# The last pair's V in 2 KB pieces on P's own partitions, P copied in two instructions, w_down in 2 KB pieces

## The chip, the core and the metric

The kernel runs on one core of a Trainium2 chip. The metric is device time in microseconds of one execution, lower is better; the time before is the median of three runs. All times inside a profile are counted from the span's start. TensorE (PE) multiplies, PEld is its weight load, VectorE (DVE), ScalarE (ACT) and GpSimd (POOL) compute, SyncE (SP) issues the DMAs.

## The reference

Two identical layers of decoding for four sequences with one new token each: a layer norm, attention with 32 query heads over 8 key/value heads and a cache of 4096 positions, then a layer norm and a gated MLP. The caches are the same in both layers.

```python
# B=4, D=512, Hq=32, Hkv=8, Sk=4096, Dh=128, F=1792, all bf16
def _A_ref(x, k_cache, v_cache, wq, wo):
    q = (x @ wq).reshape(B, Sq, Hq, Dh).transpose(0, 2, 1, 3)
    k = jnp.repeat(k_cache, 4, axis=1)
    v = jnp.repeat(v_cache, 4, axis=1)
    scores = jnp.einsum("bhqd,bhkd->bhqk", q, k) * (Dh ** -0.5)
    p = softmax(scores)
    o = jnp.einsum("bhqk,bhkd->bhqd", p, v)
    return o.transpose(0, 2, 1, 3).reshape(B, Sq, Hq * Dh) @ wo

def _B_ref(x, w_gate, w_up, w_down):
    h = sigmoid(x @ w_gate) * (x @ w_up)
    return h @ w_down

x = A_x
for _ in range(2):
    x = x + _A_ref(layernorm(x), A_k_cache, A_v_cache, A_wq, A_wo)
    x = x + _B_ref(layernorm(x), B_w_gate, B_w_up, B_w_down)
return x
```

## The kernel before

**Units and pairs.** One unit of attention is one layer, one sequence and one key/value head; there are 64, taken in pairs of two neighbouring heads, so 32 pairs (0 to 31). `ORDER` fixes the sequence of the pairs; the MLP of a sequence and its queries for the second layer (`pass_steps`) are strewn between the pairs at the places of `PLACES`. K and V of a unit are 1 MB each and lie in one of 12 slots of 128 partitions x 8 KB. Some K and V stay in their slots for the second layer (`RET`); the rest is loaded again, 98 loads in all.

**Loads.** All loads are issued by SP, in the order of `LOADS`, by `pump` (L382) as far as slots are free. Partition p of a slot gets the 32 cache rows 32p to 32p+31, one run of 8 KB (L402). The weights' loads are `wparts` (L363, issued at L388): w_o in eight parts, w_gate and w_up in four each, w_down in two parts of 7 x 128 rows, where partition p gets rows 128k + p, so that each run is one row of 1 KB. A wait of SP for a slot stands in its queue ahead of all later loads.

**One pair on the engines.** The main loop (L1172) runs over steps k = 0 to 32; step k computes the scores and the softmax of pair k and, behind it, the product with V of pair k - 1. The engines take their instructions in the order in which the loop emits them. For a pair g:
- `k_turn` (L848): DVE transposes the unit's K in its slot. `scores` (L863): PE multiplies with the queries into one PSUM bank, so that the scores of both units lie in 128 partitions x 256 columns.
- `smax` (L886, L890): DVE takes the maximum over the columns. `spread_max` (L897): PE spreads it. `softmax`: DVE reduces it over the partitions (L906, with a read of its accumulator), ACT takes the exponential (L914) into `pe`, POOL splits the sums (L928).
- `sums` (L937) and `inverse` (L947) give the reciprocal sums of the pair before.
- `ptrans`: PE transposes P into the bank `PT` (L959). There, of the 32 runs of 8 positions on a group of partitions, position (x, a) does not lie on the partition that holds its V row, so 16 copies of 32 partitions x 64 columns (x = 0 to 3, a = 0 to 3) move it: from partitions 32x to partitions 32a. For pairs 0 to 30 all 16 are ACT's (L982, into `pT`). For pair 31 the eight with x even are ACT's and the eight with x odd are DVE's (L974, into `pT_last`, which lies in a free slot): four of them at once, four put off into `later` until after the normalisation of pair 30.
- `pv` (L999): 32 products with V for each unit, eight behind each x. `pv_last` (L1027) does both units of pair 31 in one, 64 products, in the order of x; it waits for both V's slots and for the copies of each x.
- `normalise` (L1059): DVE multiplies the output by the reciprocal sums. `wo_mm` (L1077) and `wo_add` (L1097): the product with w_o, added to x.

At the end of step 30 stand the transposes and copies of pair 30's P, then the first scores of pair 31. Step 31 emits, in this order: the second scores of pair 31, `sums(30)`, `smax(31)`, one w_o product, `spread_max(31)`, `softmax(31)`, `inverse(30)`, `pv(60)`, `ptrans(31)`, `pv(61)`, `normalise(30)`. Step 32: `sums(31)`, `inverse(31)`, `pv_last`, the w_o product of pair 30, `normalise(31)`, the w_o product of pair 31.

**The MLP.** `wide_mm` (L676) computes gate or up transposed: the 128 hidden rows of block fc come out on the 128 partitions, from 128 columns of w_gate or w_up as stationary operand, four products for each block, 14 blocks. `down` (L795) and, in the last MLP, `down_rows` (L1299) multiply with w_down block by block; row p of block fc must be partition p of w_down's block fc. The last MLP, for all four sequences at once, follows the last w_o product: the layer norm (L507 to L555), `x_rows` (L1276), gate and up (112 products), the tanh, `down_rows`, and the output.

Of the kernel before, what the change touches and what calls it, by code (L numbers as in the profile page):

```python
# [6 lines left out]
ACTF = mybir.ActivationFunctionType  # L7
# [83 lines left out]
    "vkkvkkkkvv", "kkvkvvv", "kvk", "", "kvkvvvvkvvk", "", "kvkv", "",  # L91
    "", "kkvkvvkkkkvvkv", "kkvvv", "", "", "vvkkkvkkv", "", "vkvkv",
    "vvv",
)


# [110 lines left out]
def bass_interleave_layers__gqa_block_cached__glu_gated_glu__decode_kernel(  # L207
# [15 lines left out]
    REP = HQ // HKV  # L223
# [126 lines left out]
    for k, kinds in enumerate(LOADS):  # L350
        for o in range(2):
# [5 lines left out]
            if 2 * k + o >= 3 and w_small:  # L357
# [9 lines left out]
                         A_wo[n * REP * P:(n + 1) * REP * P, :].rearrange("(h p) n -> p h n", p=P)),  # L367
        "wg": lambda n: (wg_sb[:, n, :], B_w_gate[n * P:(n + 1) * P, :]),
        "wu": lambda n: (wu_sb[:, n, :], B_w_up[n * P:(n + 1) * P, :]),
        "wd": lambda n: (wd_sb[:, n * KH:(n + 1) * KH, :],  # L370
                         B_w_down[n * KH * P:(n + 1) * KH * P, :].rearrange("(k p) n -> p k n", p=P)),
    }
    assert KF == 2 * KH
    wkeys = {"wg": [f"wg{k}" for k in range(KD)], "wu": [f"wu{k}" for k in range(KD)], "wd": ["wd0", "wd1"]}
# [3 lines left out]

    def take():
        return free.pop(0)  # L380

    def pump():  # L382
        while loads:
            kind, n = loads[-1]
            if kind in wparts:
                loads.pop()
                dst, src = wparts[kind](n)
                S.dma("sp", (lambda dst, src: lambda e: e.dma_start(dst, src))(dst, src), f"wo{n}" if kind == "wo" else kind, writes=[f"{kind}{n}"])  # L388
                continue
            if not free:  # L390
                return
            loads.pop()
            s = take()
            _, b, u = seq[n]
            if kind == "k":
                where["kn", n] = s
                src = A_k_cache[b, u].rearrange("(p j) d -> p (j d)", p=P)
            else:
                where["v", b, u] = s
                src = A_v_cache[b, u].rearrange("(p j) d -> p (j d)", p=P)  # L400
            dst = slot[s][:, :]
            S.dma("sp", (lambda dst, src: lambda e: e.dma_start(dst, src))(dst, src), f"d{s}", writes=[f"s{s}"])  # L402
# [267 lines left out]
    def wide_mm(nb, which, f0, f1, M, mk):  # L670
        wsb, keys = ((wg_sb, wkeys["wg"]), (wu_sb, wkeys["wu"]))[which]
        fns = []
        for fc in range(f0, f1):
            for k in range(KD):
                fns.append(
                    (lambda fc, k: lambda e: e.matmul(  # L676
                        M[:, 64 + fc * nb:64 + (fc + 1) * nb],
                        lhsT=wsb[:, k, fc * P:(fc + 1) * P],
                        rhs=xc_bf[:, k, 0:nb],
                        start=(k == 0),  # L680
                        stop=(k == KD - 1),
                    ))(fc, k)
                )
        S.group("pe", fns, reads=["xcb"] + keys, writes=[mk])
# [264 lines left out]
            writes=[f"rden{p}"],  # L949
        )  # L950

    later = []

    def ptrans(g):
        p = g % 2
        fns = []
        for j in range(2):
            fns.append(
                (lambda j: lambda e: e.matmul(  # L959
                    PT[:, j * P:(j + 1) * P], lhsT=pe_sb[p][:, j, :], rhs=ident_bf[:, :], start=True, stop=True  # L960
                ))(j)
            )
        S.group("pe", fns, reads=["pe0"] + IDENT, writes=["PT"])
        pT = pT_last if g == NP - 1 else pT_sb[p]
        src = PT[:, 0:256].rearrange("p (n a h) -> p n a h", n=16, h=REP)
        late = g == NP - 1
        for x in range(XJ):
            for a in range(4):
                dst = pT[32 * a:32 * a + 32, x, :, :, :].rearrange("p j n h -> p (j n) h")
                frm = src[32 * x:32 * x + 32, :, a, :]  # L970
                key = f"q{x}" if late else f"pT_{x}"
                if late and x % 2:
                    later.append((
                        (lambda dst, frm: lambda e: e.tensor_copy(dst, frm))(dst, frm),  # L974
                        ["PT"],
                        [key if a == 3 else f"{key}_{a}"],
                    ))
                    if x == 1:
                        dve(*later.pop())
                else:  # L980
                    act(
                        (lambda dst, frm: lambda e: e.activation(dst, frm, ACTF.Copy))(dst, frm),  # L982
                        reads=["PT"],
                        writes=[key if a == 3 else f"{key}_{a}"],
                    )

    def pv(i):
        l, b, u = seq[i]
        g, ul = divmod(i, 2)
        p = g % 2  # L990
        s = where["v", b, u]
        pT = pT_last if g == NP - 1 else pT_sb[p]
        vv = slot[s].rearrange("p (j d) -> p j d", d=DH)
        for x in range(XJ):
            fns = []
            for c in range(4):
                for j in range(2):
                    fns.append(
                        (lambda x, c, j: lambda e: e.matmul(  # L999
                            O_ps[p][:, ul * REP:(ul + 1) * REP],  # L1000
                            lhsT=vv[:, x * JG + c * 2 + j, :],
                            rhs=pT[:, x, j, 2 * c + ul, :],
                            start=(x == 0 and c == 0 and j == 0),
                            stop=(x == XJ - 1 and c == 3 and j == 1),
                        ))(x, c, j)
                    )
            key = f"q{x}" if g == NP - 1 else f"pT_{x}"
            rd = [f"s{s}", key] + [f"{key}_{a}" for a in range(3)]
            if ul == 0 and x == 0:
                S.group("pe", fns, reads=rd, writes=[f"O{p}"])  # L1010
            else:
                S.last_write[f"O{p}"] = S.group("pe", fns, reads=rd)
        if l == 1 or not kept("v", i):
            free.append(where.pop(("v", b, u)))

    def pv_last(g):
        p = g % 2
        l, b, u = seq[2 * g]
        ss = [where.pop(("v", b, u + ul)) for ul in range(2)]
        for x in range(XJ):  # L1020
            fns = []
            for ul in range(2):
                vv = slot[ss[ul]].rearrange("p (j d) -> p j d", d=DH)
                for c in range(4):
                    for j in range(2):
                        fns.append(
                            (lambda x, c, j, ul, vv: lambda e: e.matmul(  # L1027
                                O_ps[p][:, ul * REP:(ul + 1) * REP],
                                lhsT=vv[:, x * JG + c * 2 + j, :],
                                rhs=pT_last[:, x, j, 2 * c + ul, :],  # L1030
                                start=(x == 0 and ul == 0 and c == 0 and j == 0),
                                stop=(x == XJ - 1 and c == 3 and j == 1),
                                skip_group_check=True,
                            ))(x, c, j, ul, vv)
                        )
            rd = [f"s{s}" for s in ss] + [f"q{x}"] + [f"q{x}_{a}" for a in range(3)]
            if x == 0:
                S.group("pe", fns, reads=rd, writes=[f"O{p}"])
            else:
                S.last_write[f"O{p}"] = S.group("pe", fns, reads=rd)  # L1040
        free.extend(ss)

    partner = {(0, 2): (1, 0), (0, 3): (1, 1), (1, 3): (1, 2)}
# [81 lines left out]
    fresh = {}  # L1125
    for b in range(Bn):
        n = vstep[last[0, b]] - 1
        for (o, w), st in zip(PLACES[b], pass_steps(b)):
            steps.setdefault((n + o, w), []).append(st)
        fresh[1, b] = n + PLACES[b][-1][0]  # L1130
        first = min(pos[1, b, u] for u in range(HKV)) // 2
        assert n + PLACES[b][-1][0] < first, (b, n, first)
# [39 lines left out]
    for k, (sg, vg) in enumerate(plan):  # L1172
        if sg == NP - 1:
# [5 lines left out]
            x_w = fin[:, 3 * P:4 * P].rearrange("p (c w) -> p c w", c=KD)  # L1179
            o_row = slot[tail][:, 8 * P:9 * P]  # L1180
            h_w = slot[tail][:, 9 * P:9 * P + KF * 32].rearrange("p (k w) -> p k w", w=32)
            pT_last = slot[tail][:, 14 * P:16 * P].rearrange("p (x j n h) -> p x j n h", x=XJ, j=2, n=8)
            S.inst("pool", lambda e: e.memset(slot[tail][:, 6 * P:13 * P], 0.0), writes=[f"s{tail}", "idf", "x_w", "h_w", "rs_m"])
            S.inst("pool", lambda e: e.tensor_copy(rs_m, ident_bf[:, 0:32:8]), reads=IDENT, writes=["rs_m"])
            for n in range(1, 4):
# [58 lines left out]
        if vg is not None:  # L1244
            if sg is not None:
                pv(2 * vg + 1)
                pump()
            else:
                pv_last(vg)
                early = wo_ready(k)[:1]  # L1250
                for g in early:
                    waiting.remove(g)
                    wo_mm(g, (vg + 1) % 2)
            normalise(vg)
            if sg is None:
                for g in early:
                    wo_add(g, (vg + 1) % 2)
            while later:
                dve(*later.pop(0))
            normed[seq[2 * vg]] = k  # L1260
        do_steps(k, 6)
        if sg is not None and sg != NP - 1:
# [123 lines left out]
```

## Time and profile before

| | us |
|---|---|
| median of three runs (313.06, 313.73, 314.20) | 313.73 |
| the profiled execution, whole | 313.97 |
| its span, first to last instruction | 312.2 |
| PE busy | 218.2 (70%) |
| DVE busy | 174.7 (56%) |
| ACT busy | 133.6 (43%) |
| ACT: the 32x64 copies of P, 496 of them | 106.4 |

117.43 MB come in through 21,968 packets, 376 GB/s over the span. A row of the timeline gives the start in us, the time from the first start to the last end in us, engine, line, operation, what is written from what, the tile's shape, how many instructions are merged, and in brackets how long the engine was idle before and who ended that. A row of the view by stretches gives the stretch, its length, the busy time (and instructions) of PE, PEld, DVE, ACT and POOL, the granted TensorE clock, the DMA engines' busy share and GB/s. The DMA view's first counts are cumulative: "under 2 KB" includes "under 512 B".

### The profile page before, as it was taken

To read this page: it belongs to the slowest core of one execution; us is meant where nothing else is said; L and a number is where in the kernel's file an instruction comes from. 1 tells how busy PE (TensorE), PEld (TensorE's weight loads), DVE (VectorE), ACT (ScalarE), POOL (GpSimd) and SP (SyncE) were. 2 spreads that over 40 slices of the span, in tenths; PEclk is the share of its full clock that TensorE was granted. 3 is DMA by queue.
4 is the path that set the end of the run, shared out by engine and by line. 5 is a ranking of instruction groups with operands and counts; after the bars stand their busy time and mean duration, and the time that the engine had idled before them with its cause. 6 is when DMAs were issued, how large, how long until landed. Compare 5 with 4: busy or idle time off the path is not lost. (4 is left out here: it accounts for less than half of the span.)

```text
span 312.2 us, 12055 instructions
## 1 busy us (share of the span) xinstructions
PE 218.2 (70%) x5196; PEld 160.2 (51%) x5196; DVE 174.7 (56%) x440; ACT 133.6 (43%) x588; POOL 25.8 (8%) x106
## 2 busy tenths in 40 slices
PE   1326301573349988787998877789777869988886
PEld 0313101352238566466846555665554658466676
DVE  4468220736138457974643995653886548326643
ACT  0022300545041555775156674524555741566730
POOL 0001000000000001100001000000100000020200
PEclk9999999999999999999999999999755555575555
DMA  7999999999998999999999999999999996999900
GB/s 289 427 421 388 384 405 419 422 418 378 390 400 347 415 409 420 420 418 410 352 371 341 421 423 420 418 419 418 419 420 418 417 386 244 389 345 425 401 17 3
DMA packets 21968, 117.43 MB, mean 376 GB/s; under 512 B 1944, under 2 KB 7836, under 8 KB 8860
## 3 DMA queue, kind: packets, MB, share of 16 engines
q1 hardware_dynamic: 21916, 116.67, 93.4%
q8 instruction: 41, 0.67, 0.9%
q14 instruction: 11, 0.09, 0.1%
HBM read 116.66 MB, written 0.00 MB: 374 GB/s over the span
## 5 line engine op out<-in xcount | busy, mean ns | idle before, releaser
L982 ACT ACTIVATE pT<-PT 32x64 bf16<-32x64 f32 x496 | 106.4, 214 | 82.4 <-PE PT L959 71.0
L848 DVE STREAM_TRANSPOSE slot<-slot 128x1024 f32<-128x1024 f32 (+1 forms) x63 | 109.9, 1748 | 24.7 <-DMA slot<-in_A_k_cache_dram 24.5
L999 PE MATMUL O_ps<-pT,slot 128*128 128x4 bf16 x1984 | 63.6, 167 | 43.2 <-DMA slot<-in_A_v_cache_dram 35.1
L999 PEld LDWEIGHTS O_ps<-pT,slot 128*128 128x128 bf16 x1984 | 60.5, 105 | 49.1 <-DMA slot<-in_A_v_cache_dram 35.7
L863 PE MATMUL S_ps<-slot,qz 128*32 128x256 bf16 x1024 | 64.4, 403 | 11.2 <-DVE slot L848 6.5
L863 PEld LDWEIGHTS S_ps<-slot,qz 128*32 128x32 bf16 x1024 | 29.2, 125 | 27.4 <-DVE slot L848 8.3
L914 ACT ACTIVATE pe<-S_ps,small 128x256 bf16<-128x256 f32 x32 | 15.1, 473 | 42.8 <-issue 24.4
L928 POOL TENSOR_TENSOR small<-small 128x1 f32<-128x1 f32 x64 | 12.3, 193 | 238.6 <-ACT pe L914 236.1
L1059 DVE TENSOR_TENSOR oT<-O_ps,rden 128x8 bf16<-128x8 f32 x32 | 5.3, 165 | 37.3 <-PE O_ps L999 36.1
L1077 PE MATMUL O_ps<-oT,wo 128*128 128x2 bf16 (+1 forms) x640 | 20.0, 165 | 6.1 <-DMA wo<-in_A_wo_dram 4.5
L1077 PEld LDWEIGHTS O_ps<-oT,wo 128*128 128x128 bf16 x640 | 18.7, 104 | 7.7 <-issue 6.6
L886 DVE TENSOR_REDUCE small<-S_ps 128x1 f32<-128x256 f32 x32 | 12.9, 404 | 13.2 <-PE S_ps L863 13.2
L906 DVE CUSTOM_DVE_ANT_0 junk<-MS,mask_f,small 128x128 bf16<-128x128 f32 x32 | 10.8, 338 | 11.3 <-PE MS L897 10.3
L897 PE MATMUL MS<-ident_bf,small 128*128 128x128 bf16 x64 | 12.5, 299 | 5.3 <-DVE small L890 5.3
L959 PE MATMUL PT<-ident_bf,pe 128*128 128x128 bf16 x64 | 11.9, 289 | 4.9 <-ACT pe L914 4.9
L660 POOL TENSOR_TENSOR qz<-qc,small 128x128 bf16<-128x128 bf16 x32 | 12.6, 399 | 32.9 <-ACT qc L646 32.9
L746 PE MATMUL M_ps<-wq,xc_bf 128*1 128x512 bf16 x128 | 14.7, 623 | 0.0
L937 PEld LDWEIGHTS MS<-head_b,small 128*128 128x128 bf16 x96 | 5.0, 107 | 12.6 <-issue 12.6
L897 PEld LDWEIGHTS MS<-ident_bf,small 128*128 128x128 bf16 x64 | 4.2, 108 | 14.1 <-DVE small L890 6.6
L1097 DVE TENSOR_TENSOR xT<-xT,O_ps 128x8 f32<-128x8 f32 (+1 forms) x20 | 3.2, 158 | 14.2 <-PE O_ps L1077 14.1
L646 ACT ACT_TABLE_LOAD x1 | 1.3, 1283 | 21.4 <-PE M_ps L635 21.4
L676 PEld LDWEIGHTS M_ps<-xc_bf,wg 128*128 128x128 bf16 x280 | 8.9, 107 | 0.4 <-DVE xc L520 0.4
(83 smaller groups left out, 160.3 us busy)
## 6 DMA issues: line engine op xcount, KB each, us to landing
slot<-in_A_v_cache_dram SPq DMA_DIRECT2D x51, 1024.0 KB, 10.7
slot<-in_A_k_cache_dram SPq DMA_DIRECT2D x47, 1024.0 KB, 11.2
wq<-in_A_wq_dram SPq DMA_DIRECT2D x4, 1024.0 KB, 7.6
wo<-in_A_wo_dram SPq DMA_DIRECT2D x8, 512.0 KB, 14.0
wg<-in_B_w_gate_dram SPq DMA_DIRECT2D x4, 448.0 KB, 10.1
wu<-in_B_w_up_dram SPq DMA_DIRECT2D x4, 448.0 KB, 12.1
wd<-in_B_w_down_dram SPq DMA_DIRECT2D x2, 896.0 KB, 22.2
row<-in_A_x_dram SPq DMA_DIRECT2D x1, 4.0 KB
```

Of the source, the lines that this page charges most:

```text
L660: lambda e: e.tensor_tensor(qz_sb[z][:, :, 0:4 * REP].rearrange("p i (a r) -> p i a r", r=REP), qc_sb[:, b, u:u + 2, :, :].rearrange("p u ...
L746: (lambda k, st: lambda e: e.matmul(M_ps[h][32 * st:32 * st + 1, :], lhsT=xc_bf[:, k, 0:1], rhs=wv[:, k, h, :, st, :], start=(k == 0), sto ...
L848: dve(lambda e: e.transpose(kf, kf), writes=[f"s{st}"])
L863: (lambda t, b2, e_, w0, s: lambda e: e.matmul(S_ps[p][32 * s:32 * s + 8 * REP, 0:2 * P], lhsT=qzf[:, w0:w0 + 8 * REP], rhs=ktv[:, :, s, : ...
L886: lambda e: e.tensor_reduce(m, S_ps[p][:, 0:2 * P], AX.X, ALU.max),
L897: (lambda n, col: lambda e: e.matmul(MS[:, 0:P], lhsT=top(col).broadcast_to([P, P]), rhs=ident_bf[:, :], start=(n == 0), stop=(n == 1)))(n ...
L914: lambda e: e.activation(pe_sb[p].rearrange("p j m -> p (j m)"), S_ps[p][:, 0:2 * P], ACTF.Exp, bias=nm_sb[p], scale=exp_scale, accum_out= ...
L928: (lambda n: lambda e: e.tensor_tensor(sm_sb[p][n + 1], sm_sb[p][n], top(sm_sb[p][n]), ALU.subtract))(n),
L959: (lambda j: lambda e: e.matmul(PT[:, j * P:(j + 1) * P], lhsT=pe_sb[p][:, j, :], rhs=ident_bf[:, :], start=True, stop=True))(j)
L982: (lambda dst, frm: lambda e: e.activation(dst, frm, ACTF.Copy))(dst, frm),
L999: (lambda x, c, j: lambda e: e.matmul(O_ps[p][:, ul * REP:(ul + 1) * REP], lhsT=vv[:, x * JG + c * 2 + j, :], rhs=pT[:, x, j, 2 * c + ul, ...
L1077: (lambda c, r: lambda e: e.matmul(O_ps[p][:, 64 + 2 * c:64 + 2 * c + nb], lhsT=wo_sb[:, u * REP + r, c * P:(c + 1) * P], rhs=oT_sb[n][:, ...
```

## The change

It has four parts.

- The load of the last two units' V (units 62 and 63, pair 31) is cut into four DMAs each, a = 0 to 3. Partition 32x + k gets, in quarter a of its slot, the eight cache rows from 1024a + 32k + 8x on, one run of 2 KB. These are the positions whose P comes out of the transposes on that partition. Each piece has a semaphore of its own (those that w_o's parts used).
- With that, `ptrans(31)` copies `PT` to `pT_last` without moving it: partitions 0 to 63 by ACT, 64 to 127 by DVE, 64 x 256 each. `pv_last` runs unit by unit and piece by piece, and waits for both copies and for the piece. The put-off copies (`later`) go away.
- A table `SHARE`, one entry for each pair 0 to 30, says how many of x = 1 and x = 3 are copied by DVE in `ptrans`: none, except for pair 30, where it is both, eight copies by ACT and eight by DVE.
- w_down is loaded in pieces of two neighbouring rows, 2 KB, in one part of 8 blocks and one of 6. Row i of partition p in the pair of blocks j is then row 256j + 2p + i, and `wide_mm` takes its 128 columns of w_gate and w_up at a step of two accordingly, for every MLP.

```diff
+SHARE = (
+    0, 0, 0, 0, 0, 0, 0, 0,
...
+    0, 0, 0, 0, 0, 0, 2,
 )
@@
-        "wd": lambda n: (wd_sb[:, n * KH:(n + 1) * KH, :],
-                         B_w_down[n * KH * P:(n + 1) * KH * P, :].rearrange("(k p) n -> p k n", p=P)),
+        "wd": lambda n: (wd_sb[:, 8 * n:min(KF, 8 * n + 8), :].rearrange("p (j i) n -> p j (i n)", i=2),
+                         B_w_down[8 * n * P:min(KF, 8 * n + 8) * P, :].rearrange("(j p i) n -> p j (i n)", p=P, i=2)),
@@
+    def v_parts(s, n):
+        _, b, u = seq[n]
+        rows = A_v_cache[b, u].rearrange("(a k x j) d -> a x k (j d)", a=4, k=32, x=XJ)
+        for a in range(4):
+            dst = slot[s][:, a * JG * DH:(a + 1) * JG * DH]
+            S.dma(
+                "sp",
+                (lambda dst, src: lambda e: e.dma_start(dst, src))(dst, rows[a]),
+                f"wo{4 * (n % 2) + a}",
+                writes=[f"v{n % 2}_{a}"] + ([f"s{s}"] if a == 0 else []),
+            )
@@ pump
                 where["v", b, u] = s
+                if n >= NU - 2:
+                    v_parts(s, n)
+                    continue
@@ wide_mm
-                        lhsT=wsb[:, k, fc * P:(fc + 1) * P],
+                        lhsT=wsb[:, k, bass.ds(2 * P * (fc // 2) + fc % 2, P, step=2)],
@@ ptrans
-        pT = pT_last if g == NP - 1 else pT_sb[p]
+        if g == NP - 1:
+            act(lambda e: e.activation(pT_last[0:64, :], PT[0:64, 0:2 * P], ACTF.Copy), reads=["PT"], writes=["q0"])
+            dve(lambda e: e.tensor_copy(pT_last[64:P, :], PT[64:P, 0:2 * P]), reads=["PT"], writes=["q1"])
+            return
+        pT = pT_sb[p]
...
-                if late and x % 2:
-                    later.append((
+                key = f"pT_{x}"
+                wr = [key if a == 3 else f"{key}_{a}"]
+                if x in (1, 3)[:SHARE[g]]:
+                    dve(
                         (lambda dst, frm: lambda e: e.tensor_copy(dst, frm))(dst, frm),
...
@@ pv_last
-        for x in range(XJ):
-            fns = []
-            for ul in range(2):
-                vv = slot[ss[ul]].rearrange("p (j d) -> p j d", d=DH)
-                for c in range(4):
+        pT = pT_last.rearrange("p (j n a h) -> p j n a h", j=2, a=4, h=REP)
+        for ul in range(2):
+            vv = slot[ss[ul]].rearrange("p (a s j d) -> p a s j d", a=4, s=4, j=2)
+            for a in range(4):
+                fns = []
+                for s in range(4):
                     for j in range(2):
...
-                                lhsT=vv[:, x * JG + c * 2 + j, :],
-                                rhs=pT_last[:, x, j, 2 * c + ul, :],
...
+                                lhsT=vv[:, a, s, j, :],
+                                rhs=pT[:, j, 2 * s + ul, a, :],
...
-            rd = [f"s{s}" for s in ss] + [f"q{x}"] + [f"q{x}_{a}" for a in range(3)]
...
+                rd = [f"v{ul}_{a}", "q0", "q1"]
@@ main loop, behind normalise
-            while later:
-                dve(*later.pop(0))
```

## The prediction

> **What bounds the kernel now.** I read first the page's 40 slices, then busy time by stretch, the timeline of the last 20 us, and two stretches of the DMA view.
>
> ```profile
> DMA  7999999999998999999999999999999996999900
> ```
> ```profile
> 283.00:296.00 13.00, 11.08 (x277) 8.47 (x278) 9.57 (x20) 9.91 (x46) 2.92 (x11) 0.50 1.00 418
> ```
> ```profile
> 87.81 1.02 PE L999 MATMUL O_ps<-pT,slot 128*128 128x4 bf16 x32 [7.05 <-DMA slot<-in_A_v_cache_dram]
> ```
> ```profile
> 252.98 1.01 PE L999 MATMUL O_ps<-pT,slot 128*128 128x4 bf16 x32 [1.40 <-DMA slot<-in_A_v_cache_dram]
> ```
> The DMA engines are full in 35 of 40 slices: the load of the caches sets the pace, and PE waits for V, last for 1.40 us at 252.98. From there on the view of waits names no load; the engines' own chain runs to the end, beside a DMA that is still full (share 1.00, 418 GB/s) until 296. The last step of that chain, in order of time:
>
> ```profile
> 274.27 0.17 PEld L635 LDWEIGHTS M_ps<-qT,ident_bf 128*32 128x32 bf16 x16 [0.38 <-DVE qT L785]
> ...
> 291.33 2.26 DVE L848 STREAM_TRANSPOSE slot<-slot 128x2048 f32<-128x2048 f32 x1
> ...
> 292.81 3.80 ACT L982 ACTIVATE pT<-PT 32x64 bf16<-32x64 f32 x16 [0.86 <-PE PT L959]
> ...
> 293.52 0.13 DVE L1059 TENSOR_TENSOR oT<-O_ps,rden 128x8 bf16<-128x8 f32 x1
> ...
> 294.83 0.42 DVE L886 TENSOR_REDUCE small<-S_ps 128x1 f32<-128x256 f32 x1 [1.19 <-PE S_ps L863]
> 295.29 0.16 DVE L890 TENSOR_TENSOR small<-small 128x1 f32<-128x1 f32 x1
> 295.67 0.37 PE L897 MATMUL MS<-ident_bf,small 128*128 128x128 bf16 x2
> 296.47 0.08 DVE L906 DVE_READ_ACCUMULATOR2_ANT small<- 128x1 f32 x1
> 296.63 0.47 ACT L914 ACTIVATE pe<-S_ps,small 128x256 bf16<-128x256 f32 x1
> 297.25 0.40 PE L959 MATMUL PT<-ident_bf,pe 128*128 128x128 bf16 x2 [0.22 <-ACT pe L914]
> 297.44 1.04 PE L999 MATMUL O_ps<-pT,slot 128*128 128x4 bf16 x32
> 297.69 1.88 ACT L982 ACTIVATE slot<-PT 32x64 bf16<-32x64 f32 x8 [0.49 <-PE PT L959]
> 298.34 0.22 PE L937 MATMUL MS<-head_b,small 128*128 128x8 bf16 x3
> 299.09 1.84 PE L1027 MATMUL O_ps<-slot,slot 128*128 128x4 bf16 x64 [0.53 <-ACT slot L982]
> 306.11 1.57 PEld L676 LDWEIGHTS S_ps<-xc_bf,wu 128*128 128x128 bf16 x56
> ```
> Three things are to be seen. The last product with V (L1027) starts when P is copied, not when PE is free. The last exponential at 296.63 is held by two engines at once: ACT has its 16 copies done at 296.61, and DVE's chain (maximum at 294.83, its spread on PE at 295.67, the read at 296.47 ending at 296.55) is ready about 0.09 later, the gap that stands at the exponential of 291.38, where ACT was free. And DVE is idle for only 1.19 us before the maximum at 294.83.
>
> **w_down in 2 KB pieces.** Two stretches price small packets:
> ```profile
> DMA packets 1036, 1.04 MB, mean 348 GB/s; under 512 B 17, under 2 KB 1036, under 8 KB 1036
> ```
> ```profile
> DMA packets 402, 2.92 MB, mean 417 GB/s; under 512 B 47, under 2 KB 47, under 8 KB 47
> ```
> The first (76 to 79 us) holds 1 KB packets alone, the second (55 to 62 us) 8 KB packets and the 4 B semaphore writes. With 16 engines a 1 KB packet costs 16 x 1024 / 348 = 47.1 ns of one engine, an 8 KB packet 16 x 8192 / 417 = 314.3 ns; a straight line between them is 9 ns plus 0.0373 ns per byte, so 85 ns for 2 KB, a size that the trace does not show. w_down is 1792 packets of 1 KB now, 1792 x 47.1 / 16 = 5.27 us, and 896 of 2 KB afterwards, 896 x 85 / 16 = 4.77 us: **0.50 us less DMA time**. Bounds: nothing (the stream absorbs it), and 0.87 us (2 KB as fast as 8 KB: 1.835 MB at 417 GB/s is 4.40 us). It reaches the end only if what follows hangs on the queue. It does: PE waits 7.05 us for a V behind w_down (87.81), and each later wait for V is longer than 0.5 us, the last being the 1.40 us at 252.98. I take the whole 0.50. The issues stay two.
>
> **The last pair's V.** Two transfers of 128 packets of 8 KB (256 x 314.3 / 16 = 5.03 us) become eight of 128 packets of 2 KB (1024 x 85 / 16 = 5.44 us): +0.41 us, and 96 more semaphore writes (16 for each of six more DMAs). SP issues six more DMAs at 0.33 us, 2.0 us on its queue from 281.69; nothing but the output stands behind them, and about 12 us of data is queued. Issue times and times to landing put the last three V's at 293.3, 295.8 and 298.2 us. The last pair's eighth piece would land at about 298.7, and PE wants it only after 56 of L1027's 64 products, 1.5 us after their start near 299. **Nothing on the path**; without that cover it costs 0.41.
>
> In a sentence apart: the Trainium skill, "DMA: Bandwidth & Descriptors", section "Rules for kernel authors", asks for at least 1 MiB in each DMA and its fit charges about 2 us to each; by that six more DMAs would be an estimated 12 us, but here three 1 MB loads in flight land 2.5 us apart, which is 1.05 MB / 2.5 us = 420 GB/s with nothing charged between them.
>
> **Two copies of P instead of sixteen.** ACT's 32x64 copy takes 0.214 us and its 128x512 copy (L759) 0.682; 256 columns lie at 0.42 between them. DVE's are 0.223 and 0.751 (L766): 0.45. The partitions are lanes in both pairs of rows, so I leave them out; the bounds are those rows. P is then complete at 297.69 + 0.45 + 0.05 = 298.19, not 299.09. PE has pv (L999) and the sums (L937, three at 27 ns from 298.34) ahead of it, so L1027 could start at 298.43: **0.66 us earlier** than 299.09, if nothing before moves. DVE's last copies, until 299.88, go away; nothing waited there.
>
> **SHARE: eight of pair 30's sixteen copies go from ACT to DVE.** ACT is done at 292.81 + 8 x 0.237 = 294.7, worth nothing since DVE sets the exponential as well. On DVE the copies come behind the normalisation (293.52, next start 0.20 later) and ahead of the maximum: eight at 0.25 us (four L974 copies span 0.96) is 293.72 to 295.74. They do not fit the 1.19 us gap: the maximum starts 0.91 us later. PE was busy until 295.64 with w_o, so of this 0.17 is slack: L897 starts at 295.29 + 0.91 + 0.16 + 0.05 = 296.41 instead of 295.67, **0.74 us later**, and with it the exponential, the transposes and pv, which stand behind it in order. L1027 then starts at 298.43 + 0.74 = 299.17 against 299.09: the two edits together are **+0.08 us**. Bounds: -0.66 (no delay) and +0.74 (delay, and the start not freed).
>
> **Weights read at a step of two.** L676 runs 112 times in the tail and on the path. Now 56 loads take 1.57 us with 104 ns each, (1.57 - 0.10) / 55 = 26.7 ns apart. The one load with that step is L635: 32 columns, 16 of them in 0.17 us at 102 ns each, 4.5 ns apart, 18 ns for the four that make 128 columns. So the step shows no price, and I take **0**. The other bound: the slowest 128-column loads are float32 (L507), two in 0.50 us at about 0.3, so 0.2 apart; with half the bytes an estimated 0.1 us, 112 x (0.100 - 0.027) = +8.2 us in the tail.
>
> In a sentence apart: the Trainium skill, "TensorE: Matmul & The Clock Gate", section "Weight-path perf modes", has fast loads read 32 bits at a time, two bf16, but lists the pattern as packed or strided; a step of two at half the pace would be an estimated 112 x 27 ns = 3.0 us, the list's reading nothing, and L635 agrees with the list as far as 32 columns go.
>
> **Sum.** -0.50 + 0.08 = -0.42 us. The profiled execution took 313.97 (span 312.2), so 313.55; against the runs' median of 313.73 it is **313.3**. Profiled run and median differ by 0.24, within the runs' 313.06 to 314.2. From no change this measurement tells about 0.3%, 0.94 us.
>
> **Rivals.**
> - *DVE has room* (faster). If the gap before the maximum is 2.0 us rather than 1.19, since the shifted loads move PE's scores against DVE's transpose (291.33), the delay vanishes: -0.50 - 0.66 gives **312.6**. For it: the chain of waits names ACT's copies ahead of the exponential. Against: the scores that end the gap wait for that transpose, so they move together. 0.26.
> - *The saving is lost* (same). The queue runs dry at 98 and 258 to 262 us for want of slots; if the engines set those moments, only +0.08 is left: **313.8**. Against: the waits for V above. 0.12.
> - *Strided loads lose their pace* (slower). It decides as soon as L676's loads stand more than 27 ns apart; at 0.1 us the tail alone gives 313.3 + 8.2 = **321.5**, and the pass at 257.36 and 260.00, behind the last wait for V, as much again. For it: no 128-column load with a step is in the trace; against: L635. 0.12.
> - *Pieces are paid one by one* (slower). The last load's bytes thin out over some 2.2 us (296.0 to 298.2). Paid for each of six more pieces, 13 us would put the last landing at 311.4 and L1027's end some 10 us later: **324**. Against: the 2.5 us spacing. 0.04.
> - That w_down or V are not cut as said would show as 1 KB packets left beyond w_o's 4096.
>
> **How the numbers follow.** My forecast has 0.46 (own range 312.8 to 314.3). Within 0.3%: it and the lost saving, less 0.03 for scatter upwards, 0.55. Faster: 0.26. Slower: 0.12 + 0.04 + 0.03 = 0.19. The range goes from -0.87 - 0.66 = 312.2, less some scatter, to +0.74 = 314.5 plus the runs' 0.5: 312.0 to 315.0, and leaves out the two slow rivals, 0.16.
>
> **What would show it.** 5892 packets of 1 KB (the page's 7836 under 2 KB less 1944 under 512 B) become 4100. The maximum (L886's row) of the last pair follows DVE's eight copies without a gap, and the exponential starts about 3.9 us after the normalisation before it, against 3.1 now. The last product with V starts behind the sums without waiting. The strided loads stand 26.7 ns apart. I am wrong if the tail from L1027 on is longer than 13.3 us (312.2 - 299.09 is 13.1 now), if PE waits for a V piece, or if the maximum starts on the scores' end.

## The result, and the profile after

The changed kernel takes 327.04 us (median of six runs, 325.81 to 328.40). The kernel before took 314.25 us in the six runs beside it. The ratio is 1.0408, with a 95% interval of 1.0378 to 1.0437. The change costs 12.8 us. The prediction, 313.3 us with a range up to 315.0, was wrong.

The profiled execution took 328.34 us, with a span of 326.3. Line numbers have moved: the exponential is L937, the maximum L909, the product with V L1022, the last product with V L1051, the w_o product L1100, gate and up L699. The page's slices of 8.2 us show the place at once. Below are PE, the DMA engines' share and GB/s of the kernel after.

```profile
PE   1425204455189898779988776887788689977146
...
DMA  7999999999998999999999999999999889992210
GB/s 298 428 422 384 393 404 421 419 417 391 393 411 325 414 420 425 414 419 357 351 380 420 419 422 419 394 407 367 422 423 419 306 303 359 393 385 106 102 47 3
```
Up to the 36th slice (294 us) the DMA engines are full, as before. Then there are two slices in which they are busy for 0.2 of their time and move 106 and 102 GB/s, and in the same slices PE is down to 0.7 and 0.1. Before, the loads were at full speed until 296 us and done by 298.3. The view of waits of the kernel after has a row that did not exist:

```profile
PE O_ps L1051 <- DMA slot<-in_A_v_cache_dram: 12.0, 6, 2.2
```
PE waits six times for V, 2.2 us at the longest and 12.0 us in all. The timeline of the kernel after shows these waits, and ahead of them the softmax of the last pair:

```profile
294.83 0.13 DVE L1082 TENSOR_TENSOR oT<-O_ps,rden 128x8 bf16<-128x8 f32 x1
294.99 2.00 DVE L999 CAST pT<-PT 32x64 bf16<-32x64 f32 x8
297.02 0.42 DVE L909 TENSOR_REDUCE small<-S_ps 128x1 f32<-128x256 f32 x1
...
298.58 0.47 ACT L937 ACTIVATE pe<-S_ps,small 128x256 bf16<-128x256 f32 x1 [2.57 <-DVE small L929]
...
299.63 0.38 ACT L986 ACTIVATE slot<-PT 64x256 bf16<-64x256 f32 x1 [0.49 <-PE PT L980]
299.63 0.43 DVE L987 CAST slot<-PT 64x256 bf16<-64x256 f32 x1 [1.02 <-PE PT L980]
...
300.36 0.57 PE L1051 MATMUL O_ps<-slot,slot 128*128 128x4 bf16 x16
...
301.89 0.37 PE L1051 MATMUL O_ps<-slot,slot 128*128 128x4 bf16 x8 [0.96 <-DMA slot<-in_A_v_cache_dram]
...
304.48 0.38 PE L1051 MATMUL O_ps<-slot,slot 128*128 128x4 bf16 x8 [2.22 <-DMA slot<-in_A_v_cache_dram]
...
314.78 0.37 PE L1051 MATMUL O_ps<-slot,slot 128*128 128x4 bf16 x8 [2.19 <-DMA slot<-in_A_v_cache_dram]
...
315.02 1.84 PE L1100 MATMUL O_ps<-oT,wo 128*128 128x2 bf16 x64
```
The last product with V starts at 300.36, close to where it stood (299.09). It then does sixteen products and stands still before each further piece, until 315.02 instead of 300.80: 14.2 us. Of these, 12.0 are the waits and 1.3 the later start; the remaining 0.9 or 1.0 is the product's own work, now in seven stretches. (This execution was 1.3 us late already at the normalisation of pair 30, 294.83 instead of 293.52; the medians differ by 12.8 us.) After 315.02 the tail is what it was.

Here is the DMA view of the same kernel from 302 to 314 us, when only V's pieces are on the way. The last column of the queue's row is its share of 16 engines' time.

```profile
DMA packets 591, 1.17 MB, mean 98 GB/s; under 512 B 19, under 2 KB 19, under 8 KB 591
...
q1 hardware_dynamic: 591, 1.17, 25.2%
```
A quarter of 16 engines is four. The records of semaphores say the same. This is when the semaphores of the pieces rose after their issue (us):

```
piece 1  295.69 295.86 296.07 296.68
piece 2  298.28 298.43 298.65 299.26
piece 3  300.86 301.02 301.22 301.84
...
piece 8  313.75 313.92 314.13 314.74
```
There are four landings for each piece, where every other cache load has 16. Pieces stand 2.58 us apart. With four engines a piece is 32 packets of 2 KB on each, so a packet took 2.58 / 32 = 80.6 ns, and the trace's own mean for 2 KB packets in this stretch is 84 ns, close to the prediction's 85. Its price was right; 4 engines carried it instead of 16.

The page itself has the count that tells:

```profile
DMA packets 21840, 117.43 MB, mean 360 GB/s; under 512 B 1944, under 2 KB 6044, under 8 KB 8988
```
The packets under 512 B are 1944, as before. The prediction had 96 semaphore writes more, 16 for each of six more DMAs. Two loads with 16 writes went and eight with 4 came, which leaves the count as it was; e4 below, whose eight pieces have 16 each, counts 2040.

The Trainium skill, "DMA: Bandwidth & Descriptors", section "Why a DMA increments its semaphore by 16 and not by 1", gives the rule: a transfer runs on the largest number of engines up to 16 that divides the slowest dimension of size over 1 on both sides. The source of a piece is written x, k, (j d), and x is 4. The landings above agree with the rule, and so do the runs below with 4, 8 and 128 there.

### The profile page after: what moved, and what is told of

The parts are those of the page before. It is cut to its first block, busy times and chain, and to the rows that moved or that the text cites. A ratio compares the mean times of both kernels' runs of the same rounds, so it can differ in the third digit from the quotient of the medians.

```text
span 326.3 us, 12048 instructions
## 1 busy us (share of the span) xinstructions
PE 219.5 (67%) x5196; PEld 160.2 (49%) x5196; DVE 174.9 (54%) x441; ACT 131.1 (40%) x573; POOL 25.9 (8%) x106
## 2 busy tenths in 40 slices
DMA packets 21840, 117.43 MB, mean 360 GB/s; under 512 B 1944, under 2 KB 6044, under 8 KB 8988
## 4 chain that ended last, share of the span: by engine, by line
PE 34%; DMA 31%; SPq 16%; DVE 11%; issue 5%; ACT 2%; POOL 0%; DVEq 0%; ACTq 0%
DMA slot<-in_A_v_cache_dram 19%; SPq L408 9%; PE O_ps L1022 8%; PE S_ps L886 8%; DMA slot<-in_A_k_cache_dram 7%; DVE slot L871 6%; DMA wo<-in_A_wo_dram 5%; PE M_ps L769 4%; SPq L425 4%; PE O_ps L1100 3%; SPq L397 2%; PE M_ps L699 2%; ACT pT L1005 2%; PE M_ps L530 2%; PE M_ps L818 1%
## 5 line engine op out<-in xcount | busy, mean ns | idle before, releaser
L1005 ACT ACTIVATE pT<-PT 32x64 bf16<-32x64 f32 x488 | 105.0, 215 | 82.9 <-PE PT L980 71.7
L1022 PE MATMUL O_ps<-pT,slot 128*128 128x4 bf16 x1984 | 63.4, 167 | 44.5 <-DMA slot<-in_A_v_cache_dram 36.6
L1022 PEld LDWEIGHTS O_ps<-pT,slot 128*128 128x128 bf16 x1984 | 60.3, 105 | 50.2 <-DMA slot<-in_A_v_cache_dram 37.9
L937 ACT ACTIVATE pe<-S_ps,small 128x256 bf16<-128x256 f32 x32 | 15.2, 474 | 44.7 <-issue 22.0
L1100 PE MATMUL O_ps<-oT,wo 128*128 128x2 bf16 (+1 forms) x640 | 19.9, 165 | 4.7 <-DMA wo<-in_A_wo_dram 4.4
L1100 PEld LDWEIGHTS O_ps<-oT,wo 128*128 128x128 bf16 x640 | 18.6, 104 | 6.2 <-issue 5.1
L909 DVE TENSOR_REDUCE small<-S_ps 128x1 f32<-128x256 f32 x32 | 12.9, 404 | 12.2 <-PE S_ps L886 12.2
L1051 PE MATMUL O_ps<-slot,slot 128*128 128x4 bf16 x64 | 2.8, 168 | 12.0 <-DMA slot<-in_A_v_cache_dram 12.0
L1120 DVE TENSOR_TENSOR xT<-xT,O_ps 128x8 f32<-128x8 f32 (+1 forms) x20 | 3.2, 158 | 12.8 <-PE O_ps L1100 12.7
```

The source lines that it names most:

```text
L909: lambda e: e.tensor_reduce(m, S_ps[p][:, 0:2 * P], AX.X, ALU.max),
L937: lambda e: e.activation(pe_sb[p].rearrange("p j m -> p (j m)"), S_ps[p][:, 0:2 * P], ACTF.Exp, bias=nm_sb[p], scale=exp_scale, accum_out= ...
L1022: (lambda x, c, j: lambda e: e.matmul(O_ps[p][:, ul * REP:(ul + 1) * REP], lhsT=vv[:, x * JG + c * 2 + j, :], rhs=pT[:, x, j, 2 * c + ul, ...
L1100: (lambda c, r: lambda e: e.matmul(O_ps[p][:, 64 + 2 * c:64 + 2 * c + nb], lhsT=wo_sb[:, u * REP + r, c * P:(c + 1) * P], rhs=oT_sb[n][:, ...
```

## The experiments

The theory (A): the pieces are slow because the outermost dimension of their source is 4, so that four engines carry them. The rivals: (B) each of the many DMAs costs a fixed time, as the prediction's fourth rival had it; (C) some other part of the change, the copies on DVE, w_down's pieces or the weights' step, loses the time. Two further questions came up: what SHARE costs, and what had held the last product with V in the kernel before.

### Everything but the pieces: e1

The kernel before, with w_down in 2 KB pieces, the step of two and SHARE; V whole and P in sixteen copies as before.

```diff
@@ after, undone
-                if n >= NU - 2:
-                    v_parts(s, n)
-                    continue
@@ ptrans, of the last pair: sixteen copies again; pv_last as before
```

> The changed kernel with the last pair's V loaded whole again (two loads of 1 MB, 8 KB runs) and with the sixteen copies of P of the kernel before; w_down in 2 KB pieces, the step of two in the weights and DVE's eight copies of pair 30's P stay. Theory A (a load whose source access pattern has 4 as its outermost count runs on 4 of the 16 DMA engines, so each V piece of 256 KB takes 2.58 us): the loss is all in the V pieces, so 313.5 to 314.8 us, the last product with V starting at P's copies, some 0.7 us later than before. Theory B (each V piece pays a fixed 2.2 to 2.6 us, whatever its pattern): the same. If w_down or SHARE had a part in the loss, above 316.

Three rounds: 313.87 us, ratio 0.9978 (0.9944 to 1.0013). The whole loss is gone, so C falls (the two copies of P, which e1 leaves out too, are in e4). The timeline of this kernel:

```profile
297.00 0.47 ACT L922 ACTIVATE pe<-S_ps,small 128x256 bf16<-128x256 f32 x1 [2.58 <-DVE small L914]
...
298.04 1.88 ACT L996 ACTIVATE slot<-PT 32x64 bf16<-32x64 f32 x8 [0.48 <-PE PT L967]
```
The exponential stands 3.75 us behind the normalisation (293.25 in the same view), as in the kernel after and not 3.11 as before: SHARE's delay comes without the pieces.

### Two large DMAs with the same source pattern: e2

On top of e1, V in two DMAs of 1 MB, 8 KB runs, but with x outermost.

```diff
                 src = A_v_cache[b, u].rearrange("(p j) d -> p (j d)", p=P)
+                if n >= NU - 2:
+                    src = A_v_cache[b, u].rearrange("(k x j) d -> x k (j d)", k=32, x=XJ)
```

> As e1, but the last pair's two loads of 1 MB name their source rows in the order x (4), k (32): still 128 runs of 8 KB and two DMAs, only the outermost count of the source is 4 instead of 128. Leaves out: the rows of the last pair's V stand on other partitions than their P, so the output is another. Theory A: 4 engines, 32 runs of 8 KB each at 0.31 us, 10 us for each load; the last lands near 315 instead of 298.5, the last product with V starts there, 326 to 330 us; four landings are seen for each load instead of 16. Theory B: two DMAs as before, no more pieces, 313.5 to 314.8.

One round: 331.03 us, ratio 1.0529 (1.0453 to 1.0606). PE's row in the timeline of this kernel:

```profile
316.54 1.84 PE L1043 MATMUL O_ps<-slot,slot 128*128 128x4 bf16 x64 [16.13 <-DMA slot<-in_A_v_cache_dram]
```
Its DMA view from 302 to 314 us, to be set beside that of the kernel after:

```profile
DMA packets 152, 1.20 MB, mean 100 GB/s; under 512 B 6, under 2 KB 6, under 8 KB 6
...
q1 hardware_dynamic: 152, 1.20, 23.9%
```
Two DMAs in 8 KB packets are as slow as eight in 2 KB packets: 100 against 98 GB/s, 24% of the engines. Each has four landings (the last at 306.45 and 316.29). Neither the number of DMAs nor the packet's size is the matter. B falls, and the outermost 4 does it alone.

### Eight DMAs with 128 outermost: e4

The pieces, the two copies and all else as in the change, but each piece takes 128 neighbouring runs in order; the exponential writes its columns in the order that this needs.

```diff
-        rows = A_v_cache[b, u].rearrange("(a k x j) d -> a x k (j d)", a=4, k=32, x=XJ)
+        rows = A_v_cache[b, u].rearrange("(a p j) d -> a p (j d)", a=4, p=P)
@@ softmax, pair 31
-                pe_sb[p].rearrange("p j m -> p (j m)"),
-                S_ps[p][:, 0:2 * P],
+                pe_sb[p].rearrange("p j (k x) -> p j x k", x=XJ),
+                S_ps[p][:, 0:2 * P].rearrange("p (j x k) -> p j x k", j=2, x=XJ),
```

> The changed kernel, with the last pair's exponential written in another order of its columns, so that P of position (k, x) comes out on partition 4k + x instead of 32x + k; the V piece a then is 128 partitions in order, outermost count 128 instead of 4. Eight DMAs of 256 KB with 2 KB runs as in the changed kernel. Theory A: 16 engines, no wait for V, the last product with V starts behind the sums: 327.04 less the 12.9 us that the V pieces held it, 313.5 to 314.5 us. Theory B: 326 to 329 us, unchanged.

Three rounds: 314.12 us, ratio 0.9985 (0.9952 to 1.0018). Eight DMAs of 256 KB, with 16 landings each, come 0.67 us apart (391 GB/s), the last at 299.33; PE waits for none. The change's form with another order of the source takes the kernel back to where it was, and no further.

### Eight outermost: e5

```diff
+        rows = A_v_cache[b, u].rearrange("(a z y j) d -> a y z (j d)", a=4, y=8, z=16)
```

> The changed kernel, with the source rows of each V piece named in the order y (8), z (16), so that the outermost count is 8 instead of 4; piece, run and number of DMAs stay. Leaves out: the rows of the last pair's V stand on other partitions than their P, so the output is another. Theory A (the engines that a load runs on follow the source's outermost count): 8 engines, 16 packets of 2 KB each, about 1.3 us for a piece instead of 2.58, the last landing near 304.5, 317 to 319 us; 8 landings for each piece. If only the full 128 spreads and all else is served by 4: 326 to 329. If 4 alone is bad: 313.5 to 314.8.

One round: 317.47 us, ratio 1.0109 (1.0072 to 1.0146). Two of the stretches of the last product with V in its timeline:

```profile
301.42 0.37 PE L1051 MATMUL O_ps<-slot,slot 128*128 128x4 bf16 x8 [0.91 <-DMA slot<-in_A_v_cache_dram]
302.72 0.38 PE L1051 MATMUL O_ps<-slot,slot 128*128 128x4 bf16 x8 [0.93 <-DMA slot<-in_A_v_cache_dram]
```
Its DMA view from 296 to 303 us, the queue's row:

```profile
q1 hardware_dynamic: 650, 1.25, 46.2%
```
Eight landings for each piece, and pieces 1.29 us apart; PE waits about 0.9 us four times. So 4, 8 and 128 outermost, which is 4, 8 and 16 engines, give 2.58, 1.29 and 0.67 us for 256 KB: each doubling of the engines about halves the time. That settles A.

### Pieces by x onto 32 partitions: e3

Cut the other way: one DMA for each x, 32 partitions, with k = 32 outermost.

```diff
+        rows = A_v_cache[b, u].rearrange("(a k x j) d -> x k a (j d)", a=4, k=32, x=XJ)
+        for x in range(XJ):
+            dst = slot[s][32 * x:32 * x + 32, :].rearrange("p (a c) -> p a c", a=4)
```

> The changed kernel with the V pieces cut the other way: four DMAs of 256 KB for each unit, one for each x, onto 32 partitions with four runs of 2 KB; the same bytes, the same runs, the same eight DMAs, outermost count 32; both products wait for all four pieces of their unit. Theory A: 16 engines, the last lands near 299, 313.5 to 314.8 us. Theory B: eight pieces at 2.5 us, 326 to 329 us as the changed kernel. A third possibility, that a load onto 32 partitions reaches fewer ports and runs at about half the rate: the last lands near 304, 317 to 320 us.

One round: 318.21 us, ratio 1.0121 (1.0037 to 1.0206). Each piece has 16 landings, yet the pieces land on average 1.13 us apart, 232 GB/s. The first unit's V was whole at 299.22, but the last product began 2.4 us later. Its row in the timeline is below, with e9.

### P's order made in the scores, SHARE 1: e6

e4's loads, with K's columns read in another order by the scores instead of by the exponential, and only four of pair 30's copies on DVE.

```diff
-            rhs=ktv[:, :, s, :, b2, :, e_].rearrange("p x j k -> p j x k"),
+            rhs=ktv[:, :, s, :, b2, :, e_].rearrange("p x j k -> p j k x" if g == NP - 1 else "p x j k -> p j x k"),
@@ SHARE, pair 30
-    0, 0, 0, 0, 0, 0, 2,
+    0, 0, 0, 0, 0, 0, 1,
```

> The changed kernel with V pieces whose outermost count is 128, as in e4, but with P's order made in the last pair's scores (PE reads K's columns in the order k, x) instead of the exponential's output, which took 0.83 us instead of 0.47 in e4; and SHARE 1 instead of 2 for pair 30 (four copies on DVE, which fit its gap). Exponential 0.47 us, the maximum starts at the scores' end, not behind DVE's copies; 312.8 to 314.0 us, 0.3 to 0.8 us under e4. If PE pays for the wider step in K, the scores of the last pair take longer than 1.04 us for 16 products and the gain is gone.

Five rounds: 313.81 us, ratio 0.9983 (0.9952 to 1.0013). No gain: PE paid for the new order of the moving operand, as its timeline shows.

```profile
292.25 3.97 PE L886 MATMUL S_ps<-slot,qz 128*32 128x256 bf16 x32
```
The 32 products of the last pair's scores took 3.97 us, against 1.90 in e9, where the order is the old one (both at a granted clock of 0.50); the maximum then waited 1.86 us for them.

### w_down alone: e7

```diff
+        "wd": ... B_w_down[8 * n * P:min(KF, 8 * n + 8) * P, :].rearrange("(j p i) n -> p j (i n)", p=P, i=2)
+                        lhsT=wsb[:, k, bass.ds(2 * P * (fc // 2) + fc % 2, P, step=2)],
```

> The kernel before with w_down in 2 KB pieces and the step of two in the weights alone. The prediction's term: 0.5 us less DMA time, which is seen at the wait for V behind w_down (87.81 before), and passes to the end: ratio 0.997 to 0.999. If the engines absorb it, 1.000. Weight loads with the step 26.7 ns apart.

Five rounds: 314.11 us, ratio 0.9983 (0.9954 to 1.0012). This does not decide, since half a microsecond is within the interval. Locally it is there. The wait for V behind w_down ends at 87.19 us in this kernel and 87.30 in the kernel after (L1022), against 87.81 before.

### What held the last product with V: e9, e10, e11, e8

e3's gap of 3.51 us and one of 0.68 in e4 had no releaser that fitted: V and P were there. In both, PE's record behind the gap is the same one counted from the start (matmuls, weight loads and PE's waits together, from 0): number 9921. Theory F: PE's instructions come in blocks of 16 KB through a DMA queue of their own, and a block came late. e9 is e3, and e10 is e4, with 96 more instructions (48 repeated transposes, each a weight load and a product) at the very start:

```diff
-    for k in range(KD):
+    for k in 13 * list(range(KD)):
```

> The loads of V by x onto 32 partitions, as in the run before with them, and 48 further transposes of x at the very start (each of the four transposes of the first layer norm's x is done 13 times instead of once, with the same result), so that every later instruction of PE stands 96 places further back in its stream. In that run the last product with V began 2.4 us after its last piece of V had landed. Theory F (PE's instructions come in blocks of 16 KB, and one came late): a block's edge no longer falls on the start of the last product with V, so L1051 begins within 0.3 us of its unit's last landing or right behind the sums (about 299.2 to 299.5), and if the block is late again the gap stands some 96 instructions earlier, about the transposes of P. Rival (what is awaited there is slow to be seen, the loads onto 32 partitions themselves): L1051 again starts 2 us or more after the last landing of its V.

> V in P's own order (128 runs side by side in each piece) with the exponential reordering its columns, and the same 48 further transposes at the start. In the run without them PE stood idle for 0.68 us before the last product with V, with P and the first pieces of V there since 297.8. Theory F: the idle time goes, L1051 follows the sums within 0.1 us. Rival (P's two copies, V or the reciprocal sums are late): 0.6 us or more idle there again.

One execution each, 319.65 and 315.63 us. First e3's timeline, PE's rows:

```profile
297.91 0.22 PE L960 MATMUL MS<-head_b,small 128*128 128x8 bf16 x3
301.64 1.94 PE L1051 MATMUL O_ps<-slot,slot 128*128 128x4 bf16 x64 [3.51 <-issue]
```
The same view of e9, with the transposes added:

```profile
301.72 0.43 PE L1022 MATMUL O_ps<-pT,slot 128*128 128x4 bf16 x10 [4.46 <-issue]
...
303.15 0.99 PE L1051 MATMUL O_ps<-slot,slot 128*128 128x4 bf16 x32
```
The same view of e4:

```profile
298.91 1.84 PE L1051 MATMUL O_ps<-slot,slot 128*128 128x4 bf16 x64 [0.68 <-DVE rden L970]
```
And of e10, e4 with the transposes added:

```profile
298.66 0.42 PE L1022 MATMUL O_ps<-pT,slot 128*128 128x4 bf16 x10 [0.90 <-issue]
...
300.09 1.85 PE L1051 MATMUL O_ps<-slot,slot 128*128 128x4 bf16 x64
...
302.58 1.47 PE L1100 MATMUL O_ps<-oT,wo 128*128 128x2 bf16 x50 [0.27 <-issue]
```
In both, the gap has left the last product with V, which now follows the sums, and stands inside an earlier product with V that waits for nothing, ten products before its end. It is again at record 9921. The second gap of e10, in the w_o product, is at record 10177, which is 256 on. F holds in both runs. The gap ends 1.4 to 1.6 us behind the end of a 16 KB packet of the instruction queue: 297.23 in e10, 300.26 in e9, 297.29 in e4.

The kernel before has the same mark. Its record 9921, the first instruction of the last product with V (a wait for the last unit's V, which had landed at 298.24), comes at 298.87, 0.48 us behind the one ahead of it and 1.37 us behind a 16 KB packet that ended at 297.50. The Trainium skill, "Runtime: NRT & Kernel Launch", section "Instruction fetch mechanics", tells of refills in blocks of 256 instructions, mostly hidden. The 256 agrees; here the edge was not always hidden, and took 0.5 us in the kernel before and up to 4.6 us (e9).

e8 is e6 with the same 48 transposes.

> As e6, with the four products of the first transposes of x issued 13 times over instead of once (48 products, 96 more PE instructions, in a stretch in which PE waits for the first loads). It asks what holds the last product with V in e4, where P and V were there and PE waited 0.6 us for nothing but its own finished work. Theory F (PE's instructions come in blocks of 16 KB, 256 instructions, over the same DMA engines, and the block that begins there came late): the gap of 0.4 to 0.7 us before the last product with V moves elsewhere and that product starts within 0.1 us of the sums or of P's copies. Rival (the wait belongs to that instruction, its semaphores): the gap stays where it is.

One round: 316.55 us, ratio 1.0062 (1.0028 to 1.0096). It was no test of F after all, since e6 already had no gap ahead of the last product with V (e6's stood in the w_o product, record 10177, 0.67 us; e8 has none). Why e8 is slower is open.

e11 is e4 with SHARE 1:

```diff
-    0, 0, 0, 0, 0, 0, 2,
+    0, 0, 0, 0, 0, 0, 1,
```

> V in P's own order with the exponential reordering its columns, and only four of pair 30's copies on DVE instead of eight (SHARE 1). By the prediction's sum for DVE four copies are 1.0 us and fit the gap before the maximum, so the maximum no longer follows a copy: the exponential comes 3.1 us behind the normalisation before it (before: 3.11, with eight copies 3.75), and the end is 0.6 us earlier than with eight, about 313.5, ratio 0.997. If the time of the maximum isn't what sets the end, 314.1 as with eight.

Five rounds: 314.53 us, ratio 0.9995 (0.9964 to 1.0026). The expected gain did not come. DVE's rows in the timeline of one execution, the fastest of the twelve (311.80 us):

```profile
290.50 0.13 DVE L1082 TENSOR_TENSOR oT<-O_ps,rden 128x8 bf16<-128x8 f32 x1
290.66 0.97 DVE L999 CAST pT<-PT 32x64 bf16<-32x64 f32 x4
292.29 0.42 DVE L909 TENSOR_REDUCE small<-S_ps 128x1 f32<-128x256 f32 x1 [0.67 <-PE S_ps L886]
```
DVE had room, as expected, but in this execution the scores were late: PE's gap at record 9665 (256 ahead of 9921) lies inside them and was 0.95 us here, against 0.47 in the kernel before. The exponential came 3.49 us behind the normalisation, a quarter of a microsecond less than with eight copies.

No kernel tried was faster than the one before by more than the interval.

## Why the prediction was wrong

**The step that failed** is "The last pair's V", with its verdict "Nothing on the path". It spread 1024 packets of 85 ns over 16 engines, 5.44 us. The packets cost 81 ns, but four engines carried them, 8 times 2.58 = 20.6 us. The pieces ended at 314.74 instead of "about 298.7". The pattern of the source stood in the diff. The kernel before had a sign of it too: the output, four rows long, has four landings behind its issue, where the caches' loads have 16. Of the signs of being wrong that the prediction named, two came: PE waits for V pieces, and from L1051 on the rest takes 25.9 us instead of at most 13.3. The issues were mis-sized too, at 0.33 us each: SP spent 20.4 us on the eight (8.6 in e4). That held nothing, since each issue ended over 11 us before its piece had landed.

**The rival that named the loss, "Pieces are paid one by one"**, had 0.04 and 324 us, which is near in size. It had the place right (PE waits for pieces) and the mechanism wrong: e2, with two DMAs, loses more than the change with eight, and e4, with eight, loses nothing. Its number was near by accident, six tails of 2.2 us against six waits of 2.0 on average. The estimate of 12 us that the prediction set beside its V term, 2 us for each of six more DMAs, is near the loss by the same accident: e4 has those six DMAs and pays nothing for them.

**SHARE** was right: predicted +0.74, measured +0.64 (the exponential 3.75 us behind the normalisation, against 3.11). The maximum at 297.02 follows the last copy directly. So the rival "DVE has room" falls: there was no room for eight copies. There was room for four (e11), which gained too little to be seen.

**Two copies of P** took 0.38 and 0.43 us, predicted 0.42 and 0.45. In the kernel after, the last product with V starts right behind the sums, as foretold. But the "0.66 us earlier" was not to be had in the kernel before. The prediction took the row's [0.53 <-ACT slot L982] for a wait for the copies, and the copies did not hold it. The four of x = 0 were done at 298.62, and PE's first instruction behind the edge came only at 298.87; from there it is 0.22 us to the first product (as in e4, 298.69 to 298.91), which is 299.09. By these records P earlier would have changed nothing at this point; in e4 P is complete at 297.80 and PE still waits until 298.69. In the kernel after, the block's packet had ended at 297.00 and PE came to this place only at 300.31, so the edge cost nothing there. Counted from pair 30's normalisation, the last product with V starts 5.53 us behind it, against 5.57 before: the two edits together came to -0.04 us, predicted +0.08. That is luck in part, since by these records most of what the copies seemed to give back was the edge.

**w_down** was right at its place: V behind it 0.51 us earlier, predicted 0.50, and 384 GB/s from 76 to 79 us, where it was 348. The prediction let it pass to the end because each later wait for V was longer than 0.5 us. That is misread: in the timeline of the kernel before, PE waits only 0.17 us for V at 135.28 and 0.25 at 250.59. That the saving reaches the end is neither shown nor excluded: e7's interval is wider, and the pace of the loads drifts from run to run by more than a microsecond (the normalisation of pair 30 at 293.52 before and 294.83 after, yet 292.30 in e4). Packets of 1 KB are 6044 - 1944 = 4100, as predicted.

**Weights at a step of two** cost nothing. The tail's row in the kernel after:

```profile
320.28 1.57 PEld L699 LDWEIGHTS S_ps<-xc_bf,wu 128*128 128x128 bf16 x56
```
56 loads take 1.57 us, as without the step, 26.7 ns apart. The list in the Trainium skill, "TensorE: Matmul & The Clock Gate", section "Weight-path perf modes", which has the pattern packed or strided and which the prediction set against "32 bits at a time", agrees at 128 columns.

## What to carry to other kernels

Before a transfer is rearranged, read the outermost dimension of both its sides and how many engines will carry it, and only then multiply packets by their price. In a profile, a DMA share that stands at a quarter or a half while an engine waits, with few landings for each transfer, is the sign; cutting by another order (here 128 runs side by side) mends it. The order that the products need must then be made elsewhere, and that has a price: 0.36 us in the exponential (e4), 2.07 us in the scores (e6). Where the row before a stall ends with "issue", or names a releaser long done, count the instructions: a gap that stays at the same number while the code moves under it, with the next such number 256 on, points at the fetch of instructions, and then removing the wait beside it gains nothing (P's copies here).

## What was not expected of the hardware

- 16 engines onto 32 partitions (e3) reached 232 GB/s, against 391 for 16 onto 128 (e4), in 2 KB runs both. The engines are busy all the while, as e3's DMA view from 295 to 301 us shows:

```profile
DMA packets 672, 1.23 MB, mean 205 GB/s; under 512 B 80, under 2 KB 80, under 8 KB 671
...
q1 hardware_dynamic: 671, 1.21, 93.4%
```
  A share of 0.93 at 205 GB/s: the packets themselves take longer, on average 150 ns for 2 KB in e3 against 87 in e4. The Trainium skill, "SBUF — State Buffer", section "Door 1: The DMA port swizzle", has the rate go by the ports that the partitions reach, and 32 neighbours reach half of them. The size agrees; no run separated it from other causes.
- The exponential with a strided output took 0.83 us (e4), against 0.47 in order (the kernel after).
- A moving operand read at a wider step made 32 products of 256 columns take 3.97 us (e6), against 1.90 (e9).
- An edge between blocks of PE's instructions costs from nothing (the kernel after) to 4.6 us (e9), by when the block's packet gets through; in e3 and e9 the packet ended at 299.76 and 300.26 while V's slow packets were on the same engines, in e4 and e10 at 297.29 and 297.23. That the slow loads delay it is likely and was not tested by itself.
